# V of a decode attention on a second DMA ring, and gate/up spread on VectorE

## The chip, the core and the metric

The kernel runs on one core of a Trainium2 chip. The metric is the device time of one execution in microseconds (us). A core has TensorE (PE) for matrix products into PSUM, VectorE (DVE), ScalarE (ACT), GpSimd (POOL) and SyncE (SP), each with its own queue of instructions, worked off in order. Transfers between HBM and the on-chip SBUF are issued as instructions of SP, ACT or POOL; each of the three has a ring of its own (q1, q10 and q0 in the profile), and all rings are served by the core's 16 DMA engines.

## The reference

One token (B = 1, Sq = 1) passes attention over a long cache and a gated feed-forward network, side by side; their sum is added to the input. All data are float32.

```python
xn = layernorm(x)                                   # x: (1, 1, 576)
q  = (xn @ wq) as 32 heads of 128                   # wq: 576 x 4096
scores = q . k_cache * 128**-0.5                    # k_cache: 32 heads x 16384 x 128
p  = softmax(scores)
o  = p @ v_cache                                    # v_cache: 32 heads x 16384 x 128
A  = o @ wo                                         # wo: 4096 x 576
g, u = xn @ w_gate, xn @ w_up                       # 576 x 4608 each
B  = (gelu(g) * u) @ w_down                         # w_down: 4608 x 576
out = x + A + B
```

The two caches hold 32 x 16384 x 128 x 4 bytes each, 268 MB; the weights are some 50 MB together.

## The kernel before

**Start.** x is normalized in one row, turned into columns by small matmuls, and copied 32 times side by side (`xnb`, `xtb`), so that `project` (L121) can compute a product in four blocks of 32 partitions: each block of 32 partitions holds the same row, a quarter of the result. wq's product is copied to `qrow`; `q_spread` (L143) spreads q of four heads over all partitions by a matmul with ones, `q_take` (L150) copies it to `qs`, one buffer for four heads. `ffn(0)` and `ffn(1)` (L158) compute gate and up: the product is copied from PSUM to a part of the tile `mix` by ScalarE (L166), and four GpSimd transfers each (L168) bring the four rows into `gu`, 36 values on each of 128 partitions. `ffn_act` (L175) computes gelu(g) * u from `gu` into `hT`.

**Heads.** K and V of one head are a tile of 128 partitions by 16384 values each, 8.39 MB. `kslot` has two buffers, `vslot` has one (L61, L64); `mix` is the first use of `vslot`, so the first V waits until gate and up have left it. All loads are issued by `nc.sync` (L68), on SP's ring, in the order of the loop at L238: K[0] in two halves, K[1], V[0], K[2], V[1], and so on to K[31], V[30]; V[31] goes to a K buffer. A load waits on its issuing queue until its buffer is free: K[h+2] for the DVE work of head h, V[h] for the products of head h-1.

For each head DVE multiplies K by q in place (L204) and sums over the 128 values of each key (L205) into `s`, one buffer. `softmax` (L207) takes the maximum over a partition on DVE (`pm`, L209), transposes it on PE (`pt`, L211), reduces it on DVE (`nm`, L213), spreads it by a matmul (`pb`, L215), copies it on ACT (`nb`, L217), and computes the exponentials on ACT (L218) into `pe`, one buffer. `pv` (L221) multiplies `pe` with V in 32 products on PE (64 matmuls in the trace, as float32 goes in two passes). Every fourth head `out_heads` (L228) gathers four heads: a copy `o4` on ACT, four matmuls, a copy.

What stands in which order on each engine, read from the built program: on PE pv(h-1), then pt(h) and pb(h), then pv(h); on DVE the multiply and the sum of head h, then pm(h), nm(h), then the multiply of head h+1; on ACT nb(h) and exp(h), with `o4` and the `qs` copy between them every fourth head. exp(h) waits for pv(h-1), which reads `pe`; the sum of head h+1 waits for exp(h), which reads `s`.

**End.** wd (36 rows of 576 a partition) is loaded in two pieces, wo (32 rows) in seven, all on SP's ring (L280 to L286). wd's first piece goes to the V buffer and waits for pv(30); its second piece and wo's first go to K[31]'s buffer, the rest of wo to V[31]'s. The output columns are summed in PSUM by `add_out` (L267), in halves of 288 columns and for the last rows in quarters of 144. The normalized heads are transposed by PE and brought to 128 partitions by a GpSimd transfer (`oT`, L299); x is loaded once more by GpSimd (`x2`, L307) and added on DVE. SP stores the result (L323).

Of the kernel before, what the change touches and what calls it, by code (L numbers as in the profile page):

```python
# [8 lines left out]
F32 = mybir.dt.float32  # L9
AF = mybir.ActivationFunctionType  # L10
ALU = mybir.AluOpType
AX = mybir.AxisListType

P = 128
H, SK, DH = 32, 16384, 128
D, DF = 576, 4608
R = SK // P
# [5 lines left out]
HALF = D // 2  # L23
HD = H * DH
QG, QB = HD // 4, 512
QS = HD // 2
FG, FB = DF // 4, 384
WD_T = DF // P
WO_T = HD // P
WD_PIECES = (28, 8)  # L30
WO_PIECES = (14, 8, 5, 2, 1, 1, 1)
WO_A = 14
WO_Q = 10
QUART = D // 4
HG = 4
PW = 4 * HG
# [4 lines left out]
def kernel(ctx: ExitStack, tc: tile.TileContext, x, k_cache, v_cache, wq, wo, wg, wu, wd, out):  # L41
    nc = tc.nc
    cpool = ctx.enter_context(tc.tile_pool(name="cpool", bufs=1))
# [9 lines left out]
    vv = v_cache.rearrange("b h (p n) d -> (b h) p (n d)", p=P)  # L53
    xf = x.rearrange("b s d -> (b s) d")
    of = out.rearrange("b s d -> (b s) d")
    wmain = {n: w[:DM].rearrange("(p j) f -> p (j f)", j=DJ) for n, w in (("q", wq), ("g", wg), ("u", wu))}
    wtail = {n: w[DM:].rearrange("d (s f) -> (d s) f", s=2) for n, w in (("q", wq), ("g", wg), ("u", wu))}
    wov = wo.rearrange("(p t) f -> p (t f)", t=WO_T)
    wdv = wd.rearrange("(p t) f -> p (t f)", t=WD_T)

    def kslot():  # L61
        return kpool.tile([P, R * DH], F32, tag="k", name="kslot")

    def vslot():  # L64
        return vpool.tile([P, R * DH], F32, tag="v", name="vslot")

    def load(dst, src):
        nc.sync.dma_start(dst, src)  # L68
        return dst

    ROW3 = 3 * DF
    wq_t, wg_t, mix = kslot(), kslot(), vslot()
    qt = load(wg_t[:, ROW3 : ROW3 + QS], wtail["q"])
    load(wq_t, wmain["q"])
    row3, tails, at = {}, {}, 0
# [4 lines left out]

    xrow = mix[:1, ROW3 + FG : ROW3 + FG + D]
    nc.scalar.dma_start(xrow, xf)

    ident = cpool.tile([P, P], F32, name="ident")
    make_identity(nc, ident)
# [3 lines left out]
    nc.vector.memset(eps_t, EPS)  # L89
    par = cpool.tile([P, 2], F32, name="par")  # L90
    nc.vector.tensor_reduce(par, ident.rearrange("p (d s) -> p s d", s=2), axis=AX.X, op=ALU.add)
    sel = cpool.tile([P, PW], F32, name="sel")
    nc.vector.tensor_reduce(sel, ident.rearrange("p (q r) -> p r q", q=4)[:, :PW, :], axis=AX.X, op=ALU.add)

    st = cpool.tile([1, 2, nc.vector.BN_STATS_DIM], F32, name="st")
    for i in range(2):
# [21 lines left out]
    xtb = cpool.tile([P, 2, 32], F32, name="xtb")  # L118
    nc.vector.tensor_copy(xtb, xt.unsqueeze(2).to_broadcast([P, 2, 32]))

    def project(steps, group, size):  # L121
        pg = ps_big.tile([P, 3, 512], F32, tag="pb", name="pg")
        for k, (j, rhs) in enumerate(steps):
            for b in range(group // size):
                for q in range(4):
                    lo = q * group + b * size
                    if j < DJ:
                        lhs = xnb[:, j, :]
                    else:
                        lhs = xtb[:, q // 2, :]  # L130
                        lo = (q % 2) * group + b * size
                    nc.tensor.matmul(pg[32 * q : 32 * q + 32, b, :size], lhs, rhs[:, lo : lo + size],  # L132
                                     start=k == 0, stop=k == len(steps) - 1)
        return pg[:, : group // size, :size]

    steps = [(DJ, qt)] + [(j, wq_t[:, j * HD : (j + 1) * HD]) for j in range(DJ)]
    pq = project(steps, QG, QB)
    qrow = cpool.tile([P, QG], F32, name="qrow")
    nc.scalar.activation(qrow.rearrange("p (b f) -> p b f", f=QB), pq, AF.Copy)  # L139

# [2 lines left out]
    def q_spread(h):  # L143
        r = 32 * (h // (H // 4))
        lo = h % (H // 4) * DH
        pq = ps_s.tile([P, 512], F32, tag="sm", name="pq")
        nc.tensor.matmul(pq, ones[r : r + 1, :], qrow[r : r + 1, lo : lo + QH * DH], start=True, stop=True)  # L147
        return pq
# [6 lines left out]

    gu = cpool.tile([P, 2, WD_T], F32, name="gu")

    def ffn(which):  # L158
        n = "gu"[which]
        t = kslot() if which else wg_t  # L160
        steps = [(3, row3[n]), (DJ, tails[n])]
        load(t[:, :ROW3], wmain[n][:, :ROW3])
        steps += [(j, t[:, j * DF : (j + 1) * DF]) for j in range(DJ - 1)]
        gc = mix[:, ROW3 + which * FG : ROW3 + (which + 1) * FG]
        pg = project(steps, FG, FB)
        nc.scalar.activation(gc.rearrange("p (b f) -> p b f", f=FB), pg, AF.Copy)  # L166
        for q in range(4):
            nc.gpsimd.dma_start(gu[32 * q : 32 * q + 32, which, :], gc[32 * q : 32 * q + 1, :])  # L168

    ffn(0)  # L170
    ffn(1)

    hT = cpool.tile([P, WD_T], F32, name="hT")

    def ffn_act():  # L175
        g, u = gu[:, 0], gu[:, 1]
        t1 = cpool.tile([P, WD_T], F32, name="t1")
        tc.keep_in_program_order(nc.vector.tensor_mul(t1, g, g))
        tc.keep_in_program_order(nc.vector.tensor_scalar(t1, t1, 0.044715, 1.0, op0=ALU.mult, op1=ALU.add))
        tc.keep_in_program_order(nc.vector.tensor_mul(t1, t1, g))  # L180
        th = cpool.tile([P, WD_T], F32, name="th")
        nc.scalar.activation(th, t1, AF.Tanh, scale=0.7978845608028654)
        t2 = cpool.tile([P, WD_T], F32, name="t2")
        tc.keep_in_program_order(nc.vector.scalar_tensor_tensor(t2, th, 1.0, g, op0=ALU.add, op1=ALU.mult))
        tc.keep_in_program_order(nc.vector.scalar_tensor_tensor(hT, t2, 0.5, u, op0=ALU.mult, op1=ALU.mult))
# [6 lines left out]
    S, KT, VT = {}, {}, {}  # L192
# [35 lines left out]
    def out_heads(h):  # L228
        o4 = spool.tile([P, 512], F32, name="o4", bufs=1)
        nc.scalar.activation(o4, PO[h // HG % 2], AF.Copy)  # L230
        pc = ps_s.tile([P, 512], F32, tag="sm", name="pc")
        pick = sel.rearrange("p (i j) -> p j i", j=4)
        for j in range(4):
            nc.tensor.matmul(pc[:, :HG], o4[:, j * DH : (j + 1) * DH], pick[:, j, :], start=j == 0, stop=j == 3)  # L234
        nc.scalar.activation(oall[:, h : h + HG], pc[:, :HG], AF.Copy)

    q_take(0, q_spread(0))
    for h in range(H + 1):  # L238
        if h < H:
            KT[h], n = kslot(), R if h else SUB  # L240
            for i in range(0, R, n):
                load(KT[h][:, i * DH : (i + n) * DH], kv[h][:, i * DH : (i + n) * DH])
        if h > 0:
            VT[h - 1] = load(vslot() if h < H else kslot(), vv[h - 1])
        more = (h + 1) % QH == 0 and h + 1 < H
        pq = q_spread(h + 1) if more else None
        if h < H:
            for i in range(0, R, n):
                qk(h, i, n)
            KT.pop(h)  # L250
        if h == 0:
            ffn_act()
        if h > 0:
            pv(h - 1)
            if h % HG == 0:
                out_heads(h - HG)
        if more:
            q_take(h + 1, pq)
        if h < H:
            softmax(h)  # L260
# [19 lines left out]
    ta, tb, te = vslot(), kslot(), kslot()  # L280
    a, b = WD_PIECES
    wd_rows = load_rows(ta, 0, wdv, 0, a) + load_rows(tb, 0, wdv, a, b)
    wo_rows, lo = [], 0
    for n in WO_PIECES:
        wo_rows += load_rows(tb, b + lo, wov, lo, n) if lo < WO_A else load_rows(te, lo - WO_A, wov, lo, n)
        lo += n  # L286
# [4 lines left out]
    nc.vector.reciprocal(rl, pl[:, :H])  # L291
    on = cpool.tile([P, H], F32, name="on")
    nc.vector.tensor_mul(on, oall, rl)
    po = ps_s.tile([P, 512], F32, tag="sm", name="pot")
    nc.tensor.transpose(po[:H, :P], on, ident)
    orow = cpool.tile([H, P], F32, name="orow")
    nc.scalar.activation(orow, po[:H, :P], AF.Copy)
    oT = cpool.tile([P, WO_T], F32, name="oT")
    nc.gpsimd.dma_start(oT, orow)  # L299

    for j, w in enumerate(wd_rows):
        add_out(half[j % 2], hT[:, j : j + 1], w)

    x2 = te[:, R * DH - 2 * HALF : R * DH - HALF]
    nc.vector.memset(x2, 0.0)
    for i in range(2):
        nc.gpsimd.dma_start(x2[32 * i : 32 * i + 1, :], xf[:, i * HALF : (i + 1) * HALF])  # L307

    for j, w in enumerate(wo_rows):
        if j < WO_T - WO_Q:  # L310
            add_out(half[j % 2], oT[:, j : j + 1], w, last=j >= WO_T - WO_Q - 2)
            continue
        if j == WO_T - 5:
            nc.vector.tensor_add(x2[:64], x2[:64], PO[0][64:, :HALF])  # L314
            nc.vector.tensor_add(x2[:64], x2[:64], acc[:64, :HALF])
            for i, g in enumerate(quart):
                r, lo = 32 * (i // 2), i % 2 * QUART
                nc.tensor.matmul(g, ones[r : r + 1, :1], x2[r : r + 1, lo : lo + QUART], start=False, stop=False)
        add_out(quart, oT[:, j : j + 1], w, last=j == WO_T - 1)

    o4 = te[:, R * DH - 3 * HALF : R * DH - 3 * HALF + QUART]
    nc.vector.tensor_copy(o4, acc4)
    nc.sync.dma_start(of.rearrange("o (a f) -> (o a) f", a=4), o4[0:P:32, :])  # L323


# [26 lines left out]
```

## Time and profile before

| | us |
|---|---|
| runs, median of 3 (lowest, highest) | 1370.02 (1369.91, 1370.03) |
| the profiled execution | 1369.89 |
| its span | 1368.1 |
| DVE busy in the span | 1128.3 |
| PE busy | 402.8 |
| ACT busy | 38.9 |
| mean rate of the transfers | 430 GB/s |

The page splits the span into 40 slices and gives the busy share of each engine in tenths; the DMA line is the mean of the 16 DMA engines. Lines of groups name a source line, an engine, the operation, the tiles written and read with their shapes, the count, the busy time and the mean of one in ns, and the idle time before it with what ended it. Lines of the timeline begin with the start and the duration in us. Lines of issues name the queue (SPq is SP's own sequencer), the transfer, its size in KB and the time from issue to landing.

### The profile page before, as it was taken

The numbers are of one execution on the slowest core, as the hardware profiler recorded it, in microseconds if no ns is written. First come the engines' busy times: TensorE is split into PE (matmuls) and PEld (weight loads), VectorE is DVE, ScalarE is ACT, GpSimd is POOL, SyncE is SP. The second block draws the span as 40 slices with busy tenths as digits, with TensorE's granted clock in tenths as the row PEclk, the third lists the DMA queues.
The fourth block names the chain that finished last, engine by engine and source line by source line (L and its number), as shares of the span: only waits on it lengthen the run. The fifth ranks groups of instructions, "written<-read, shape, count | busy, mean of one in ns | idle before, by whom it ended". The sixth has DMA issues, their size and how long they took to land.

```text
span 1368.1 us, 6409 instructions
## 1 busy us (share of the span) xinstructions
PE 402.8 (29%) x2877; PEld 117.2 (9%) x2877; DVE 1128.3 (82%) x160; ACT 38.9 (3%) x128; POOL 6.4 (0%) x17
## 2 busy tenths in 40 slices
PE   4331233322311233322212233322213333222156
PEld 1110000100000000100000000100001000000012
DVE  1059999899888888898888888998888888988840
ACT  0000000000000000000000000000000000000000
POOL 0010000000000000000000000000000000000000
PEclk8775665665566565555565665665566565665577
DMA  9999999999999999999999999999999999999997
GB/s 405 439 423 446 435 431 428 428 439 430 437 437 430 431 428 441 432 433 435 428 439 429 434 431 434 435 430 445 429 430 430 429 439 429 445 428 430 431 431 331
DMA packets 12196, 588.06 MB, mean 430 GB/s; under 512 B 1653, under 2 KB 1673, under 8 KB 2186
## 3 DMA queue, kind: packets, MB, share of 16 engines
q1 hardware_dynamic: 11816, 587.60, 99.4%
q8 instruction: 22, 0.36, 0.1%
q0 software_dynamic: 352, 0.06, 0.0%
q14 instruction: 4, 0.03, 0.0%
q10 hardware_dynamic: 2, 0.00, 0.0%
HBM read 587.60 MB, written 0.00 MB: 429 GB/s over the span
## 4 chain that ended last, share of the span: by engine, by line
DMA 68%; PE 21%; DVE 8%; another core or an unknown queue 1%; issue 1%; ACT 0%; SPq 0%; DVEq 0%; ACTq 0%
DMA vslot<-in_A_v_cache_dram 60%; PE po L225 19%; DVE kslot L204 5%; DVE s L205 3%; DMA vslot<-in_B_w_down_dram 2%; DMA kslot<-in_A_wo_dram 2%; DMA kslot<-in_A_wq_dram 2%; PE pg L132 2%; DMA kslot<-in_A_k_cache_dram 1%; PE pt L211 0%; PE pq L147 0%; ACT qrow L139 0%; DVE pm L209 0%; ACT qs L152 0%
## 5 line engine op out<-in xcount | busy, mean ns | idle before, releaser
L204 DVE TENSOR_TENSOR kslot<-kslot,qs 128x16384 f32<-128x16384 f32 (+1 forms) x33 | 551.3, 16706 | 88.7 <-DMA kslot<-in_A_k_cache_dram 88.7
L205 DVE TENSOR_REDUCE s<-kslot 128x128 f32<-128x16384 f32 (+1 forms) x33 | 551.2, 16703 | 3.3
L225 PE MATMUL po<-vslot,pe 128*16 128x512 f32 x1984 | 282.1, 732 | 645.5 <-DMA vslot<-in_A_v_cache_dram 630.1
L225 PEld LDWEIGHTS po<-vslot,pe 128*16 128x16 f32 x1984 | 66.7, 112 | 845.5 <-issue 828.5
L211 PE MATMUL pt<-ident,pm 128*1 128x128 f32 x32 | 11.9, 372 | 237.4 <-DVE pm L209 237.4
L265 DVE MEMSET acc<- 128x144 f32 x1 | 0.2, 178 | 75.9 <-ACT vslot L166 75.9
L132 PE MATMUL pg<-kslot,xnb 128*32 128x384 f32 (+1 forms) x208 | 24.6, 638 | 35.0 <-DMA kslot<-in_B_w_gate_dram 19.1
L217 ACT ACTIVATE nb<-pb 128x1 f32<-128x1 f32 x32 | 5.5, 172 | 813.4 <-PE pb L215 813.4
L314 DVE TENSOR_TENSOR kslot<-kslot,po 64x288 f32<-64x288 f32 x1 | 0.5, 456 | 29.7 <-PE po L270 29.7
L211 PEld LDWEIGHTS pt<-ident,pm 128*1 128x1 f32 x32 | 2.5, 79 | 260.8 <-DVE pm L209 221.8
L215 PE MATMUL pb<-nm,ones 1*128 1x1 f32 x64 | 18.2, 351 | 13.2 <-DVE nm L213 13.2
L213 DVE TENSOR_REDUCE nm<-pt 1x1 f32<-1x128 f32 x32 | 8.9, 279 | 15.0 <-PE pt L211 15.0
L215 PEld LDWEIGHTS pb<-nm,ones 1*128 1x128 f32 x64 | 15.9, 306 | 22.1 <-DVE nm L213 12.0
L147 PE MATMUL pq<-qrow,ones 1*128 1x512 f32 x16 | 15.6, 1073 | 0.0
L270 PE MATMUL acc<-kslot,oT 128*1 128x144 f32 (+1 forms) x124 | 11.0, 371 | 6.6 <-DMA kslot<-in_A_wo_dram 6.6
L218 ACT ACTIVATE pe<-s,nb 128x128 f32<-128x128 f32 x32 | 12.8, 401 | 1.0
L291 DVE RECIPROCAL rl<-pl 128x32 f32<-128x32 f32 x1 | 0.4, 358 | 14.7 <-PE pl L289 14.7
L132 PEld LDWEIGHTS pg<-kslot,xnb 128*32 128x32 f32 x208 | 7.4, 130 | 52.8 <-DMA kslot<-in_B_w_gate_dram 19.9
L230 ACT ACTIVATE o<-po 128x512 f32<-128x512 f32 x8 | 4.8, 597 | 221.5 <-PE po L225 221.5
L270 PE MATMUL acc<-vslot,hT 128*1 128x288 f32 x56 | 8.4, 464 | 6.5 <-DMA vslot<-in_B_w_down_dram 6.5
L225 PE MATMUL po<-kslot,pe 128*16 128x512 f32 x64 | 9.5, 758 | 2.6 <-DMA kslot<-in_A_v_cache_dram 2.6
L234 PE MATMUL pc<-sel,o 128*128 128x4 f32 x64 | 8.4, 255 | 5.7 <-ACT o L230 5.7
(74 smaller groups left out, 111.1 us busy)
## 6 DMA issues: line engine op xcount, KB each, us to landing
kslot<-in_A_k_cache_dram SPq DMA_DIRECT2D x2, 4096.0 KB, 23.0
vslot<-in_B_w_down_dram SPq DMA_DIRECT2D x1, 8064.0 KB, 29.4
kslot<-in_B_w_gate_dram SPq DMA_DIRECT2D x1, 6912.0 KB, 55.3
kslot<-in_B_w_up_dram SPq DMA_DIRECT2D x1, 6912.0 KB
kslot<-in_A_wo_dram SPq DMA_DIRECT2D x1, 4032.0 KB, 38.0
vslot<-in_B_w_gate_dram SPq DMA_DIRECT2D x1, 2304.0 KB
vslot<-in_B_w_up_dram SPq DMA_DIRECT2D x1, 2304.0 KB, 37.2
kslot<-in_B_w_down_dram SPq DMA_DIRECT2D x1, 2304.0 KB
```

The source lines that it names most:

```text
L132: nc.tensor.matmul(pg[32 * q : 32 * q + 32, b, :size], lhs, rhs[:, lo : lo + size], start=k == 0, stop=k == len(steps) - 1)
L147: nc.tensor.matmul(pq, ones[r : r + 1, :], qrow[r : r + 1, lo : lo + QH * DH], start=True, stop=True)
L204: tc.keep_in_program_order(nc.vector.tensor_mul(blk, blk, Q[h].to_broadcast([P, n, DH])))
L205: nc.vector.tensor_reduce(S[h][:, i : i + n], blk, axis=AX.X, op=ALU.add)
L211: nc.tensor.transpose(pt[:1, :P], pm, ident)
L213: tc.keep_in_program_order(nc.vector.tensor_reduce(nm, pt[:1, :P], axis=AX.X, op=ALU.max, negate=True))
L215: nc.tensor.matmul(pb[:, :1], ones[:1, :], nm, start=True, stop=True)
L217: nc.scalar.activation(nb, pb[:, :1], AF.Copy, scale=SCALE)
L218: nc.scalar.activation(pe4, S.pop(h).rearrange("p (k s) -> p k s", s=4), AF.Exp, bias=nb, scale=SCALE, accum_out=lsum[:, h : h + 1])
L225: nc.tensor.matmul(PO[h // HG % 2][q : q + PW, :], pe[:, lo : lo + PW], vt[:, k * 512 : (k + 1) * 512], start=i == 0 and k < 4, stop=i == ...
L234: nc.tensor.matmul(pc[:, :HG], o4[:, j * DH : (j + 1) * DH], pick[:, j, :], start=j == 0, stop=j == 3)
L270: nc.tensor.matmul(g, lhs, w[:, i * n : (i + 1) * n], start=id(g) not in seen, stop=last)
```

## The change

The function `load` gets the ring as an argument; V of heads 0 to 30 is issued by ScalarE's queue, all other loads stay on SP's. In the built program the issue of V[h] stands on ACT behind exp(h-1) and ahead of nb(h) and exp(h); every fourth one stands behind the copy `o4`, and the `qs` copy of every fourth head stands behind a V issue. V[h] waits for pv(h-1) as before.

Gate and up are no longer copied by ScalarE and moved by GpSimd. A mask `same` (1 where the partition's number within its block of 32 equals the column) is multiplied into the product on DVE, reading PSUM, in blocks of 11, 11 and 10 times 36 columns, and a sum over the blocks on DVE gives `gu`. `oT` is made by a mask `quarter` on DVE and a matmul with `same`. x2 is loaded at the start by two issues on ScalarE into a tile of its own, zeroed by GpSimd. wo is loaded in pieces of 16, 8, 4, 2, 1, 1 rows in place of 14, 8, 5, 2, 1, 1, 1, the quarters take the last 8 rows in place of 10, and the sums of the halves are added 4 rows before the end in place of 5. ScalarE issues the store. GpSimd issues no transfer.

```diff
-WO_PIECES = (14, 8, 5, 2, 1, 1, 1)
-WO_A = 14
-WO_Q = 10
+WO_PIECES = (16, 8, 4, 2, 1, 1)
+WO_A = 16
+WO_Q = 8
...
-    def load(dst, src):
-        nc.sync.dma_start(dst, src)
+    def load(dst, src, ring=nc.sync):
+        ring.dma_start(dst, src)
...
+    x2 = cpool.tile([P, HALF], F32, name="x2")
+    nc.gpsimd.memset(x2, 0.0)
+    for i in range(2):
+        nc.scalar.dma_start(x2[32 * i : 32 * i + 1, :], xf[:, i * HALF : (i + 1) * HALF])
...
-        gc = mix[:, ROW3 + which * FG : ROW3 + (which + 1) * FG]
         pg = project(steps, FG, FB)
-        nc.scalar.activation(gc.rearrange("p (b f) -> p b f", f=FB), pg, AF.Copy)
-        for q in range(4):
-            nc.gpsimd.dma_start(gu[32 * q : 32 * q + 32, which, :], gc[32 * q : 32 * q + 1, :])
+        gm = mix[:, ROW3 : ROW3 + FG].rearrange("p (m t) -> p m t", t=WD_T)
+        at = 0
+        for b, size in enumerate(FB):
+            m = size // WD_T
+            nc.vector.tensor_mul(gm[:, at : at + m, :], pg[:, b, :size].rearrange("p (m t) -> p m t", t=WD_T),
+                                 same[:, at : at + m].unsqueeze(2).to_broadcast([P, m, WD_T]))
+            at += m
+        nc.vector.tensor_reduce(gu[:, which, :], gm.rearrange("p m t -> p t m"), axis=AX.X, op=ALU.add)
...
-            VT[h - 1] = load(vslot() if h < H else kslot(), vv[h - 1])
+            VT[h - 1] = load(vslot() if h < H else kslot(), vv[h - 1], nc.scalar if h < H else nc.sync)
...
-    nc.tensor.transpose(po[:H, :P], on, ident)
-    orow = cpool.tile([H, P], F32, name="orow")
-    nc.scalar.activation(orow, po[:H, :P], AF.Copy)
+    nc.tensor.matmul(po[:, :WO_T], onx, same, start=True, stop=True)
     oT = cpool.tile([P, WO_T], F32, name="oT")
-    nc.gpsimd.dma_start(oT, orow)
+    nc.scalar.activation(oT, po[:, :WO_T], AF.Copy)
...
-    nc.sync.dma_start(of.rearrange("o (a f) -> (o a) f", a=4), o4[0:P:32, :])
+    nc.scalar.dma_start(of.rearrange("o (a f) -> (o a) f", a=4), o4[0:P:32, :])
```

More of the change, by code (lines that the diff above doesn't have):

```diff
@@ L26 @@
 QS = HD // 2
-FG, FB = DF // 4, 384
 WD_T = DF // P
+FG = DF // 4
+FB = (11 * WD_T, 11 * WD_T, 10 * WD_T)
 WO_T = HD // P
 WD_PIECES = (28, 8)
-WO_PIECES = (14, 8, 5, 2, 1, 1, 1)
-WO_A = 14
-WO_Q = 10
+WO_PIECES = (16, 8, 4, 2, 1, 1)
+WO_A = 16
+WO_Q = 8
 QUART = D // 4
@@ L91 @@
     nc.vector.tensor_reduce(par, ident.rearrange("p (d s) -> p s d", s=2), axis=AX.X, op=ALU.add)
-    sel = cpool.tile([P, PW], F32, name="sel")
-    nc.vector.tensor_reduce(sel, ident.rearrange("p (q r) -> p r q", q=4)[:, :PW, :], axis=AX.X, op=ALU.add)
+    same = cpool.tile([P, 32], F32, name="same")
+    nc.vector.tensor_reduce(same, ident.rearrange("p (q r) -> p r q", q=4), axis=AX.X, op=ALU.add)
+    quarter = cpool.tile([P, 4], F32, name="quarter")
+    nc.vector.tensor_reduce(quarter, ident.rearrange("p (q r) -> p q r", q=4), axis=AX.X, op=ALU.add)
     st = cpool.tile([1, 2, nc.vector.BN_STATS_DIM], F32, name="st")
@@ L119, with project @@
     nc.vector.tensor_copy(xtb, xt.unsqueeze(2).to_broadcast([P, 2, 32]))
-    def project(steps, group, size):
+    def project(steps, group, sizes):
         pg = ps_big.tile([P, 3, 512], F32, tag="pb", name="pg")
         for k, (j, rhs) in enumerate(steps):
-            for b in range(group // size):
+            for b, size in enumerate(sizes):
                 for q in range(4):
-                    lo = q * group + b * size
+                    lo = q * group + sum(sizes[:b])
                     if j < DJ:
@@ L130, in project @@
                         lhs = xtb[:, q // 2, :]
-                        lo = (q % 2) * group + b * size
+                        lo -= q // 2 * 2 * group
                     nc.tensor.matmul(pg[32 * q : 32 * q + 32, b, :size], lhs, rhs[:, lo : lo + size],
                                      start=k == 0, stop=k == len(steps) - 1)
-        return pg[:, : group // size, :size]
+        return pg
     steps = [(DJ, qt)] + [(j, wq_t[:, j * HD : (j + 1) * HD]) for j in range(DJ)]
-    pq = project(steps, QG, QB)
+    pq = project(steps, QG, (QB, QB))[:, :2, :]
     qrow = cpool.tile([P, QG], F32, name="qrow")
@@ L231, in out_heads @@
         pc = ps_s.tile([P, 512], F32, tag="sm", name="pc")
-        pick = sel.rearrange("p (i j) -> p j i", j=4)
+        pick = same[:, :PW].rearrange("p (i j) -> p j i", j=4)
         for j in range(4):
@@ L293 @@
     nc.vector.tensor_mul(on, oall, rl)
+    onx = te[:, R * DH - 2 * P : R * DH - P]
+    nc.vector.tensor_mul(onx.rearrange("p (h r) -> p h r", r=4), on.unsqueeze(2).to_broadcast([P, H, 4]), quarter.unsqueeze(1).to_broadcast([P, H, 4]))
     po = ps_s.tile([P, 512], F32, tag="sm", name="pot")
-    nc.tensor.transpose(po[:H, :P], on, ident)
-    orow = cpool.tile([H, P], F32, name="orow")
-    nc.scalar.activation(orow, po[:H, :P], AF.Copy)
+    nc.tensor.matmul(po[:, :WO_T], onx, same, start=True, stop=True)
     oT = cpool.tile([P, WO_T], F32, name="oT")
-    nc.gpsimd.dma_start(oT, orow)
+    nc.scalar.activation(oT, po[:, :WO_T], AF.Copy)
     for j, w in enumerate(wd_rows):
         add_out(half[j % 2], hT[:, j : j + 1], w)
[L304 to L307, printed above, removed]
     for j, w in enumerate(wo_rows):
@@ L312 @@
             continue
-        if j == WO_T - 5:
+        if j == WO_T - 4:
             nc.vector.tensor_add(x2[:64], x2[:64], PO[0][64:, :HALF])
```

## The prediction

> **What bounds the kernel now.** I read the page first: the busy shares, the 40 slices, the queues. The slices show what runs all the time; the queue table shows how the bytes get there.
>
> ```profile
> span 1368.1 us, 6409 instructions
> DVE  1059999899888888898888888998888888988840
> DMA  9999999999999999999999999999999999999997
> ...
> q1 hardware_dynamic: 11816, 587.60, 99.4%
> q0 software_dynamic: 352, 0.06, 0.0%
> q10 hardware_dynamic: 2, 0.00, 0.0%
> ```
>
> The transfer engines are full from the first slice to the last but one, and all of it is q1, SP's ring (q10 is ScalarE's, q0 GpSimd's). VectorE comes next. So the time is bytes over rate, as long as the ring never runs dry. One head as the timeline shows it, with the issues of SP in it:
>
> ```profile
> 1240.12 17.23 DVE L204 TENSOR_TENSOR kslot<-kslot,qs 128x16384 f32<-128x16384 f32 x1 [3.08 <-DMA kslot<-in_A_k_cache_dram]
> 1257.46 17.22 DVE L205 TENSOR_REDUCE s<-kslot 128x128 f32<-128x16384 f32 x1
> 1259.59 9.48 PE L225 MATMUL po<-vslot,pe 128*16 128x512 f32 x64 [21.91 <-DMA vslot<-in_A_v_cache_dram]
> 1269.12 0.33 SPq L68 DMA_DIRECT2D vslot<-in_A_v_cache_dram  x1
> 1274.71 0.33 SPq L68 DMA_DIRECT2D kslot<-in_A_v_cache_dram  x1
> 1274.71 0.29 DVE L209 TENSOR_REDUCE pm<-s 128x1 f32<-128x128 f32 x1
> 1275.05 0.37 PE L211 MATMUL pt<-ident,pm 128*1 128x128 f32 x1 [5.99 <-DVE pm L209]
> 1275.46 0.28 DVE L213 TENSOR_REDUCE nm<-pt 1x1 f32<-1x128 f32 x1 [0.47 <-PE pt L211]
> 1276.62 0.40 ACT L218 ACTIVATE pe<-s,nb 128x128 f32<-128x128 f32 x1
> 1278.82 17.23 DVE L204 TENSOR_TENSOR kslot<-kslot,qs 128x16384 f32<-128x16384 f32 x1 [3.08 <-DMA kslot<-in_A_k_cache_dram]
> 1298.29 8.90 PE L225 MATMUL po<-vslot,pe 128*16 128x512 f32 x64 [21.91 <-DMA vslot<-in_A_v_cache_dram]
> ```
>
> A head lasts 1298.29 - 1259.59 = 38.70 us. K and V are 8.39 MB each (128 rows of 16384 x 4 B), so the ring gives 433.5 GB/s and one tensor alone takes w = 19.35 us. DVE needs 17.23 + 17.22 + 0.1, **34.6 us** a head, and the softmax's way over PE (pm, pt, nm) 1.1 us. The single V buffer is busy with pv, landing to release, for p = 9.2 us (8.4 to 9.9 in the chain of waits). On one ring that gap costs nothing: K[h+1] stands behind V[h] in SP's queue, its bytes fill the gap, and the next V is queued long before they end. **The order on the one ring covers the gap.** Note the 5.99 us that PE waits for pm: pv(h-1) ends 5.6 us before the reduction of head h. That is all the slack V has against DVE, since on PE pt(h) stands behind pv(h-1), and on DVE the next multiply stands behind nm(h), which needs pt(h).
>
> The end of the run, from the timeline and (the wo line) the chain of waits:
>
> ```profile
> 1307.25 0.33 SPq L68 DMA_DIRECT2D vslot<-in_B_w_down_dram  x1
> 1317.63 9.47 PE L225 MATMUL po<-kslot,pe 128*16 128x512 f32 x64 [2.56 <-DMA kslot<-in_A_v_cache_dram]
> 1336.72 27.70 DMA kslot<-in_A_wo_dram
> 1364.96 0.31 DVE L322 COPY kslot<-acc 128x144 f32<-128x144 f32 x1 [4.18 <-PE acc L270]
> 1365.29 0.66 SPq L323 DMA_DIRECT2D out_dram<-kslot  x1
> ```
>
> wd is issued at 1307.25, after pv(30); V[31], landing at 1317.6, covers that. From V[31] to the last wo row 46.8 us pass for 20.05 MB, which are 46.3 at full rate. The profiled execution took 1369.89 us (the median of the runs is 1370.02), so 5.5 us lie behind the last landing at 1364.4.
>
> **The change: V on a second ring.** SP's queue keeps K[0] to K[31], V[31], wd, wo. ScalarE's queue gets V[0] to V[30], each placed behind the exp of the head before and ahead of its own head's nb and exp; it waits for pv of the head before. K no longer stands behind V, nor V behind K. How do two rings share the engines? The trace of before shows it once: the eight small gate/up transfers on q0 while q1 was full (timeline; the view of tile gu; the chain of waits).
>
> ```profile
> 67.18 16.74 SPq L68 DMA_DIRECT2D kslot<-in_A_k_cache_dram  x3
> 83.60 1.13 ACT L166 ACTIVATE vslot<-pg 128x1152 f32<-128x1152 f32 x1 [15.28 <-PE pg L132]
> 85.02 1.97 POOL L168 DMA_DIRECT2D gu<-vslot  x4 [14.27 <-ACT vslot L166]
> 101.63 0.33 SPq L68 DMA_DIRECT2D vslot<-in_A_v_cache_dram  x1
> ...
> DMA to landing us min/median/max: 6.6/9.7/14.9
> ...
> 67.18 18.31 DMA kslot<-in_A_k_cache_dram
> ```
>
> Those of 85.0 to 87.0 landed by 101.6, ahead of K[1], queued at 83.9 behind the second half of K[0] (12.6 MB from 85.5 on, 29 us): not in order of issue. Four of 32 rows are 8 rows on each of 16 engines. In 14.9 us an engine at 433.5/16 = 27.1 GB/s moves eight rows of 32 KB (K[0]'s second half, 9.7 us) and two of 64 KB (4.8): ten of SP's rows for eight of q0's. So I take **one row in turn**. K and V rows are both 64 KB, so each ring gets half. That is an estimate; q10 itself carried 2 packets, too few to show it. The bounds are 0 and 1 for V's share.
>
> The page "DMA: Bandwidth & Descriptors" of the Trainium skill, section "Issuing engines are not separate DMA queues", says that such transfers run on the same 16 engines and interleave, and that a second issuing engine saves issue time only. By it alone the sum would be no change (rival 1); the SP rows above show 0.33 us an issue, already hidden.
>
> From issue to landing I add s = 2.4 us to the bytes, from the smallest full load:
>
> ```profile
> kslot<-in_A_wq_dram SPq DMA_DIRECT2D x1, 1024.0 KB, 4.8
> ```
>
> (4.8 less 2.4 for 1.05 MB.) Rules for the walk: K[h+2] is issued when red(h) ends, V[h] when pv(h-1) ends; a transfer alone moves at full rate, two at half (V[0] against K[0]'s 32 KB rows at 2:1); mul(h) starts at nm(h-1) and K[h] landed; nm(h) 1.1 behind red(h), and 0.7 or more behind pv(h-1); pv takes 9.2. V[0] is free at 87.0: 83.6, three spreads of 0.57, 0.57 and 0.53, a reduction of 1.3, handovers (below). In us:
>
> | h | K landed | red(h) ends | V issued | V landed | pv ends |
> |---|---|---|---|---|---|
> | 0 | 106.7 | 124.1 | 87.0 | 122.3 | 136.8 |
> | 1 | 133.9 | 168.4 | 136.8 | 174.3 | 183.5 |
> | 2 | 167.2 | 204.1 | 183.5 | 216.0 | 225.3 |
> | 3 | 197.9 | 239.8 | 225.3 | 257.8 | 267.0 |
> | 4 | 233.6 | 275.4 | 267.7 | 301.0 | 310.2 |
> | 5 | 269.3 | 311.1 | 310.2 | 350.5 | 359.7 |
> | 6 | 308.8 | 346.7 | 359.7 | 390.1 | 399.3 |
> | 7 | 351.3 | 395.1 | 399.3 | 436.2 | 445.4 |
>
> K runs ahead at DVE's 35.7 us a head; V, sharing, needs 42 and falls behind. V[4] lands at 301 while K[6] is done at 308.8 and K[7] waits for red(5): the engines idle until 312.6, the first 4 us. From head 5 on pv(h-1) ends after red(h), DVE stands behind nm, and two heads repeat:
>
> - long: K[h+2] and V[h] start within some 2 us: V lands s + 2w = 41.1 us after issue, less up to 2; I take 40. Then pv, 9.2, in which the next K has the engines alone.
> - short: that K has had 12.7 us of its 19.35 before V[h+1] moves, 6.7 are left to share, so V lands s + w + 6.7 = 28.4 after issue. Then pv, 9.2, and **nothing to move**: the next K waits for a reduction that began when the long pv ended, 34.6 + 1 us before.
>
> Two heads: 40 + 9.2 + 28.4 + 9.2 + 0.3 (every fourth V stands behind the 0.6 us copy of o4) = 87.1 against 77.4, 9.7 of it idle engines. V[7] goes at 399.3; eleven pairs later V[29] at 1357.4; V[30] at 1406.6, landing 1435.0; pv(30) ends at 1444.2. V[31] has landed long before (SP issues it when red(30) ends, ahead of V[30]), so wd starts uncovered: 2.4 + 46.8 = 1493.4 for the last wo row. With 5.5 behind it: **1499 us**, 129 us over the 1369.9 of the profiled execution.
>
> **The smaller edits** do not touch that sum.
>
> ```profile
> L314 DVE TENSOR_TENSOR kslot<-kslot,po 64x288 f32<-64x288 f32 x1 | 0.5, 456 | 29.7 <-PE po L270 29.7
> 24.87 9.04 PE L132 MATMUL pg<-kslot,xnb 128*32 128x512 f32 x64 [12.55 <-DMA kslot<-in_A_wq_dram]
> ```
>
> Spreading: one DVE multiply of 288 columns from PSUM takes 456 ns and the copy of 144 at the end takes 0.31 us, so about 1.0 ns a column and 0.17 fixed: 0.57, 0.57, 0.53 us; the reduction of 1152 columns at 17.22 us for 16384 is 1.2 plus 0.1. Twice 3 us on DVE in place of two ACT copies of 1.13. The first set hides behind the load of up, the second delays K[0]'s multiply from 85.5 to 86.9; the start is bound by transfers. If that cover were gone it costs 1.4 us. The GpSimd transfers' 14.9 us were late for nothing but V[0]'s issue; V[0] leaves 15 us earlier and takes rows from K[0] and K[1], which land 11 and 19 us later than one ring would land them (95.2, 114.5). That starts the walk, and by itself costs nothing while the engines are full. oT, now by a matmul instead of a transfer, is made when the last pv ends and needed when wo's first rows land, behind 10.6 MB of wd (24 us). The x2 loads add two issues on ScalarE ahead of the square root, the selection tiles 0.6 us on DVE: the projection has 12.55 us of waiting for wq ahead of it. Either costs 0 here, and at most 1.9 (two issues of 0.66 and the 0.6) without that cover. The q copy of every fourth head now stands behind a V issue on ACT, 0.3 us late at 400, seven times. wo in six pieces ends in the same 288 KB row; one issue less lies behind 5 MB queued: -0.4 to 0. The store costs ScalarE what it cost SP, 0.66: between -0.3 and +0.3.
>
> **Rivals.**
>
> 1. *The rings do not share by halves*: V is served first or in order of issue. V keeps up if it lands within 38.7 - 9.2 - 2.4 = 27.1 us of sharing, so from a share of 19.35/27.1 = 0.71 on. Then no lag builds, the order of before comes back, and the time is 1370. For: nothing shows q10 under load. Against: the q0 rows. Chance 0.06.
> 2. *Faster*: as rival 1, and the second ring fills what the one leaves open, 0.6% of the span by q1's 99.4%: 8.2 us, so 1362. It decides from the same 0.71, in the head loop, if the open 0.6% are between transfers. For: two rings can overlap issue and landing (2.4 us). Against: 433.5 GB/s is reached throughout, with no dry stretch to fill. Chance 0.06.
> 3. *Part of it*: V's share between 0.6 and 0.71, or a softer lag. The lag then builds over more heads and the gap is partly covered: between the uncovered wd alone (9.2 + 2.4 = 11.6, so 1381) and two thirds of the gaps, 1455. Chance 0.09.
> 4. *K is favoured*, share under 0.35: the long leg grows towards s + 19.35/0.35 = 57.7 us until K blocks: 1530 to 1590. Chance 0.04.
>
> **How the numbers follow.** The forecast has 0.75. Its own range: gaps of 7 us instead of 9.7 (s of 0.5 instead of 2.4 in each) take 12 x 2.7 = 32 off: 1467; pv at 9.9 instead of 9.2 adds 0.7 x 24 = 17, and a slower shared rate some more: 1525. Held to 8 in 10 with a part of rival 3: 1450 to 1530. A measurement of this kernel tells 0.2% from no change, 2.7 us. Faster is rival 2, 0.06; the same is rival 1, 0.06; slower is the rest, 0.88.
>
> **What would show it.** q10 with 31 V tensors (260 MB); a DMA share of some 0.89 over heads 6 to 30, with dry stretches of 8 to 10 us every second head that begin when a V lands; V's time to landing alternating near 28 and 40; DVE waiting for pt at nm, some 15 us every second head; V[31] landed before V[30], and a dry stretch ahead of wd. The forecast is wrong if V lands in under 27 us every time, or if the DMA slices stay at 9 and 430.

## The result and the profile after

| | us |
|---|---|
| before, median of 4 runs | 1370.01 |
| after, median of 4 runs (lowest, highest) | 1500.32 (1497.86, 1502.82) |
| the profiled execution after | 1502.82 |
| its span | 1501.0 |

The ratio is 1.0951, 95% interval [1.0937, 1.0964]. The forecast was 1499.0 in a range of 1450 to 1530. Slices, queues and three groups of the page after:

```profile
span 1501.0 us, 6360 instructions
...
DVE  1077999995969968687897877789887877888830
DMA  9999999999797997979899898899999898999978
...
q1 hardware_dynamic: 7200, 327.55, 51.7%
q10 hardware_dynamic: 4478, 260.06, 40.1%
...
L215 DVE TENSOR_TENSOR kslot<-kslot,qs 128x16384 f32<-128x16384 f32 (+1 forms) x33 | 550.8, 16690 | 13.0 <-DMA kslot<-in_A_k_cache_dram 9.6
...
L236 PE MATMUL po<-vslot,pe 128*16 128x512 f32 x1984 | 285.5, 740 | 914.7 <-DMA vslot<-in_A_v_cache_dram 914.7
L224 DVE TENSOR_REDUCE nm<-pt 1x1 f32<-1x128 f32 x32 | 8.9, 278 | 223.2 <-PE pt L222 223.2
```

The bytes are the same, 260 MB of them now on q10. The two rings together fill 91.8% of the engines' span (51.7 and 40.1) where the one filled 99.4%. The first ten slices are still full; then sevens and eights come in. DVE's two waits in a head, as the page before has them:

```profile
L204 DVE TENSOR_TENSOR kslot<-kslot,qs 128x16384 f32<-128x16384 f32 (+1 forms) x33 | 551.3, 16706 | 88.7 <-DMA kslot<-in_A_k_cache_dram 88.7
L213 DVE TENSOR_REDUCE nm<-pt 1x1 f32<-1x128 f32 x32 | 8.9, 279 | 15.0 <-PE pt L211 15.0
```

Before, DVE waited 88.7 us in all for K and 15.0 us for pt ahead of nm. Now it waits 223 us for pt, and 13 us ahead of the multiply (L215), 9.6 of them for K. So DVE does not lack K; it waits for its turn behind PE, and PE waits 915 us for V.

A stretch of the loop in steps of 2 us (start:end, length, PE, PEld, DVE, ACT, POOL busy, PE clock, DMA share, GB/s):

```profile
1170.00:1172.00 2.00, 0.00 (x0) 0.00 (x0) 2.00 (x1) 0.00 (x0) 0.00 (x0) 0.50 1.13 492
1172.00:1174.00 2.00, 0.00 (x0) 0.00 (x0) 2.00 (x1) 0.00 (x0) 0.00 (x0) 0.50 0.16 66
1174.00:1176.00 2.00, 0.00 (x0) 0.00 (x0) 2.00 (x1) 0.00 (x0) 0.00 (x0) 0.50 0.00 0
1176.00:1178.00 2.00, 1.85 (x12) 0.56 (x16) 2.00 (x1) 0.00 (x0) 0.00 (x0) 0.50 0.00 0
1178.00:1180.00 2.00, 2.00 (x16) 0.39 (x9) 1.13 (x2) 0.00 (x0) 0.00 (x0) 0.50 0.79 262
```

The timeline of the same place:

```profile
1144.11 0.28 DVE L224 TENSOR_REDUCE nm<-pt 1x1 f32<-1x128 f32 x1 [10.19 <-PE pt L222]
1144.32 17.20 DVE L215 TENSOR_TENSOR kslot<-kslot,qs 128x16384 f32<-128x16384 f32 x1
1161.62 17.22 DVE L216 TENSOR_REDUCE s<-kslot 128x128 f32<-128x16384 f32 x1
1176.15 9.84 PE L236 MATMUL po<-vslot,pe 128*16 128x512 f32 x64 [31.26 <-DMA vslot<-in_A_v_cache_dram]
1178.87 0.33 SPq L69 DMA_DIRECT2D kslot<-in_A_k_cache_dram  x1
1178.88 0.29 DVE L220 TENSOR_REDUCE pm<-s 128x1 f32<-128x128 f32 x1
1185.91 0.27 PE L222 MATMUL pt<-ident,pm 128*1 128x128 f32 x1
1186.05 0.34 ACTq L69 DMA_DIRECT2D vslot<-in_A_v_cache_dram  x1
1186.22 0.28 DVE L224 TENSOR_REDUCE nm<-pt 1x1 f32<-1x128 f32 x1 [7.06 <-PE pt L222]
1186.43 17.20 DVE L215 TENSOR_TENSOR kslot<-kslot,qs 128x16384 f32<-128x16384 f32 x1
```

Read it downwards. The last bytes of V move at about 1172.3 (a share of 0.16 in the stretch from 1172), V has landed by 1176.0, and the K before it too; the engines have nothing. The next V has to wait for pv (to 1185.98); the next K has to wait for the reduction that runs until 1178.8. From 1172.3 to about 1178.9 nothing moves. And the reduction is late because the multiply before it began only at 1144.32, when the pv before had let pt through: nm stood 10.19 us behind pt there, stands 7.06 us behind it here, and pt behind pv. Before, a K stood in the one ring behind every V, and this hole was filled.

### The profile page after: what moved, and what is told of

The parts are those of the page before. It is cut to its first block, busy times and chain, and to the rows that moved or that the text cites. A ratio compares the mean times of both kernels' runs of the same rounds, so it can differ in the third digit from the quotient of the medians.

```text
span 1501.0 us, 6360 instructions
## 1 busy us (share of the span) xinstructions
PE 390.4 (26%) x2870; PEld 112.5 (7%) x2870; DVE 1133.9 (76%) x169; ACT 36.2 (2%) x126; POOL 1.0 (0%) x7
## 3 DMA queue, kind: packets, MB, share of 16 engines
q1 hardware_dynamic: 7200, 327.55, 51.7%
q10 hardware_dynamic: 4478, 260.06, 40.1%
## 4 chain that ended last, share of the span: by engine, by line
DMA 78%; PE 21%; DVE 0%; issue 0%; SPq 0%; ACT 0%; ACTq 0%
DMA vslot<-in_A_v_cache_dram 71%; PE po L236 19%; DMA kslot<-in_B_w_up_dram 3%; DMA kslot<-in_A_wo_dram 3%; DMA kslot<-in_A_wq_dram 2%; PE pg L139 1%; PE acc L281 1%; DVE gu L179 0%; PE pt L222 0%; DVE vslot L176 0%; SPq L69 0%; DVE x L320 0%; DVE x L321 0%; PE acc L324 0%; DVE kslot L328 0%
## 5 line engine op out<-in xcount | busy, mean ns | idle before, releaser
L215 DVE TENSOR_TENSOR kslot<-kslot,qs 128x16384 f32<-128x16384 f32 (+1 forms) x33 | 550.8, 16690 | 13.0 <-DMA kslot<-in_A_k_cache_dram 9.6
L236 PE MATMUL po<-vslot,pe 128*16 128x512 f32 x1984 | 285.5, 740 | 914.7 <-DMA vslot<-in_A_v_cache_dram 914.7
L139 PE MATMUL pg<-kslot,xnb 128*32 128x396 f32 (+2 forms) x208 | 23.8, 620 | 34.6 <-DMA kslot<-in_B_w_gate_dram 19.3
L226 PE MATMUL pb<-nm,ones 1*128 1x1 f32 x64 | 13.2, 272 | 12.6 <-DVE nm L224 12.6
L226 PEld LDWEIGHTS pb<-nm,ones 1*128 1x128 f32 x64 | 10.7, 207 | 19.1 <-DVE nm L224 13.8
L159 ACT ACTIVATE qs<-pq 128x512 f32<-128x512 f32 x8 | 4.8, 597 | 264.7 <-PE pt L222 238.8
L220 DVE TENSOR_REDUCE pm<-s 128x1 f32<-128x128 f32 x32 | 9.1, 286 | 1.1
L245 PE MATMUL pc<-same,o 128*128 128x4 f32 x64 | 8.4, 255 | 5.7 <-ACT o L241 5.7
L154 PE MATMUL pq<-qrow,ones 1*128 1x512 f32 x16 | 9.9, 700 | 0.0
```

Source lines behind the costliest of these rows:

```text
L215: tc.keep_in_program_order(nc.vector.tensor_mul(blk, blk, Q[h].to_broadcast([P, n, DH])))
L220: tc.keep_in_program_order(nc.vector.reduce_max(pm, S[h], axis=AX.X))
L226: nc.tensor.matmul(pb[:, :1], ones[:1, :], nm, start=True, stop=True)
L236: nc.tensor.matmul(PO[h // HG % 2][q : q + PW, :], pe[:, lo : lo + PW], vt[:, k * 512 : (k + 1) * 512], start=i == 0 and k < 4, stop=i == ...
```

## The experiments

The **theory** is that of the prediction: the rings move row for row, V gets half, falls behind, and from then on nothing covers the time in which pv reads the single V buffer. **Rivals**: another edit costs it; two rings cost rate by themselves; ScalarE's in-order queue, in which a waiting V issue holds up the softmax.

### Only the other edits; only the ring

```diff
-            VT[h - 1] = load(vslot() if h < H else kslot(), vv[h - 1], nc.scalar if h < H else nc.sync)
+            VT[h - 1] = load(vslot() if h < H else kslot(), vv[h - 1])
```

> The changed kernel with V back on SP's ring; all its other edits stay. If the second ring alone makes the loss, this is back at 1370, give or take 2 us (the other edits were put at -0.7 to +0.8). If the edits at the start or the end carry a part of the 130 us, that part stays: anything above 1375 would say so.

Measured: 1370.00 us (11 runs), ratio 1.0 [0.9991, 1.0009]. In the kernel before, with only V's ring changed:

```diff
-    def load(dst, src):
-        nc.sync.dma_start(dst, src)
+    def load(dst, src, ring=nc.sync):
+        ring.dma_start(dst, src)
...
-            VT[h - 1] = load(vslot() if h < H else kslot(), vv[h - 1])
+            VT[h - 1] = load(vslot() if h < H else kslot(), vv[h - 1], nc.scalar if h < H else nc.sync)
```

> The kernel before with nothing changed but V of heads 0 to 30 on ScalarE's ring. Theory of the lag (each ring moves half, V's buffer gap is uncovered, DVE stands behind PE): 1490 to 1510, as the whole change. V[0] starts some 15 us later here, at about 102 instead of 87, since gate/up still pass through GpSimd; the walk by the same rules gives 6 us more for that, so about 1505. If the other edits carried the loss: 1370.

Measured: 1513.08 us (one run), 3 us above the range that was expected. The ring is the whole loss; with V on the one ring the other edits come to nothing within 0.1%. This kernel is 13 us slower than the whole change, where 6 were expected for the later start of V[0]. Its chain of waits (V's time from issue to landing, heads 0 to 3):

```profile
101.97 42.05 DMA vslot<-in_A_v_cache_dram
152.99 33.82 DMA vslot<-in_A_v_cache_dram
196.56 42.03 DMA vslot<-in_A_v_cache_dram
248.06 28.29 DMA vslot<-in_A_v_cache_dram
```

V[0] goes at 102 instead of 87, and the pattern of a long and a short wait is there from head 2 on, three heads sooner than after the whole change. Three more heads at some 5 us would be about what it costs; no run moves the start of V[0] alone.

### How the rings share: K in halves, K in thirds

```diff
             KT[h], n = kslot(), R if h else SUB
-            for i in range(0, R, n):
-                load(KT[h][:, i * DH : (i + n) * DH], kv[h][:, i * DH : (i + n) * DH])
+            kn = min(n, R // 2)
+            for i in range(0, R, kn):
+                load(KT[h][:, i * DH : (i + kn) * DH], kv[h][:, i * DH : (i + kn) * DH])
```

> The changed kernel with each K loaded in two transfers of 8192 columns, so that SP's rows are 32 KB against V's 64 KB. If the rings take one row in turn, V gets two thirds; that is just under the 0.71 from which V keeps up, and the walk by the prediction's rules gives about 1418. If the rings share by bytes whatever the row, or if two rings simply cost rate, or if the loss comes from V's issue standing in ScalarE's queue: 1500 as before.

Measured: 1455.79 us (one run). In thirds the loop reads

```diff
+            cuts = (0, 43, 86, R) if h else (0, SUB, R)
+            for i, e in zip(cuts, cuts[1:]):
+                load(KT[h][:, i * DH : e * DH], kv[h][:, i * DH : e * DH])
```

> The changed kernel with each K loaded in three transfers of 43, 43 and 42 keys a partition, rows of 21.5 KB. One row in turn gives V three quarters, over the 0.71: no lag, no dry stretch, 1367 to 1371. If two rings cost rate by themselves (contention), it stays above 1370 by that cost, seen as a rate under 433 GB/s in a stretch without dry spells. If the rings share by bytes, or the place in ScalarE's queue makes the loss: 1500.

Measured: 1384.60 us (4 runs), ratio 1.0104 [1.0091, 1.0118]. Its control, one ring and K in thirds:

> Control for the kernel with K in thirds on two rings (1384.6 us, no dry stretch, 427 GB/s): the same three transfers for each K, but V back on SP's ring. If rows of 21.5 KB are themselves slower, it is 1383 to 1387 and the second ring costs nothing once V keeps up. If it is the taking of turns between two rings that costs rate, this is back at 1370 to 1372.

Measured: 1375.34 us (4 runs), ratio 1.0038 [1.0023, 1.0053]. That lies between the two times expected of it, so each of the two causes seems to have a part.

Shorter rows on K's ring take a third of the loss away in halves and nine tenths in thirds, so the share is not by bytes. The queues in a stretch in which both rings had work (packets, MB, share), first after the change (1188 to 1208 us), then with K in halves (139 to 160 us):

```profile
q1 hardware_dynamic: 71, 4.65, 53.7%
q10 hardware_dynamic: 64, 4.19, 48.4%
```

```profile
DMA packets 209, 9.40 MB, mean 448 GB/s; under 512 B 16, under 2 KB 16, under 8 KB 16
q10 hardware_dynamic: 94, 6.16, 67.8%
q1 hardware_dynamic: 115, 3.24, 35.9%
```

After the change every packet is a row: 71 rows against 64 of the same length. With K in halves 16 of the 209 packets are under 512 B and no rows; 3.24 MB are 99 rows of 32 KB, so it is 99 rows against 94. V's share of the bytes is 0.47 and 0.66. That it is one row in turn shows in shorter windows. By an estimate from 433.5 GB/s over 16 engines a row of 64 KB takes one engine 2.4 us, and after the change the windows of 2.4 us from 1189.0 to 1208.2 hold 16 rows of q10, then 16 of q1, and so on, eight times without an exception. The first two:

```profile
q10 hardware_dynamic: 16, 1.05, 100.8%
q1 hardware_dynamic: 16, 1.05, 100.8%
```

The loop at 440 to 1240 us, in thirds on two rings and in thirds on one:

```profile
440.00:1240.00 800.00, 223.94 (x1457) 62.28 (x1457) 710.25 (x84) 20.86 (x78) 0.00 (x0) 0.61 1.00 427
```

```profile
440.00:1240.00 800.00, 222.34 (x1454) 61.44 (x1454) 719.22 (x82) 20.21 (x75) 0.00 (x0) 0.61 1.00 430
```

The expectations for halves and thirds both missed on the slow side. With thirds, 5.3 us of the 14.6 are there on one ring already (430 in place of 433 GB/s); the other 9.3 come with the second ring (427), at a DMA share of 1.00 and thus without dry stretches. In halves the walk was 38 us short. V there takes 30 to 32 us from issue to landing in heads 2 to 6, as two thirds gives (2.4 + 29), still over the 27.1, so a lag did have to build. From V's issue at 464.7 us to the one at 1356.2 it then takes near 33 us, and a head 42.5 us, where the walk's rules have 40.6 (31.4 + 9.2). Why V takes longer there is not settled.

### ScalarE's queue

```diff
-            VT[h - 1] = load(vslot() if h < H else kslot(), vv[h - 1], nc.scalar if h < H else nc.sync)
+            VT[h - 1] = load(vslot() if h < H else kslot(), vv[h - 1], nc.gpsimd if h < H else nc.sync)
```

> The changed kernel with V of heads 0 to 30 issued by GpSimd, on q0, in place of ScalarE. ScalarE's queue holds no V issue any more, so if the softmax standing behind V's issue makes the loss, this is 1370 to 1385. If it is the lag (two rings by halves, a V buffer that leaves its ring empty while it is read), the queue that issues does not matter: 1490 to 1515.

Measured: 1508.21 us (one run), inside the range of the lag. The queue, and the loop after the change and in this kernel:

```profile
q0 software_dynamic: 4464, 260.05, 39.9%
```

```profile
440.00:1240.00 800.00, 196.41 (x1323) 53.31 (x1323) 638.35 (x74) 18.66 (x71) 0.00 (x0) 0.60 0.91 387
440.00:1240.00 800.00, 195.69 (x1323) 53.43 (x1315) 631.21 (x74) 18.88 (x71) 10.02 (x19) 0.60 0.90 386
```

The 260 MB went over q0, ScalarE issued none of it, and the loop runs at 386 GB/s where the change had 387. The place of the V issue in ScalarE's queue is not the cause.

### The gap itself

V in two transfers, with the buffer released as a whole:

```diff
-            VT[h - 1] = load(vslot() if h < H else kslot(), vv[h - 1], nc.scalar if h < H else nc.sync)
+            VT[h - 1] = vslot() if h < H else kslot()
+            vn = R // 2 if h < H else R
+            for i in range(0, R, vn):
+                load(VT[h - 1][:, i * DH : (i + vn) * DH], vv[h - 1][:, i * DH : (i + vn) * DH], nc.scalar if h < H else nc.sync)
```

> The changed kernel with each V loaded in two transfers of 32 KB rows, on ScalarE's ring; the buffer is still released as a whole. K in halves gave V 0.615 of the shared bytes, so V should get 0.385 here. pv's first half runs when the first half lands, so the ring stands empty for 4.6 + 2.4 us instead of 9.2 + 2.4. A smaller share with a smaller gap: by the walk's rules 1450 to 1495. Theory of ScalarE's queue: 1500 or above, as the queue is blocked longer.

Measured: 1467.20 us (one run), inside the expected range. The share of 0.615 in that expectation is less than the 0.66 read above; by one row in turn V in halves gets a third, not 0.385. And with one tile for all heads, so that each half is released when it has been read:

```diff
+            if h == 1:
+                vbig = vslot()
+            VT[h - 1], ring = (vbig, nc.scalar) if h < H else (kslot(), nc.sync)
+            for i in (0, SUB):
+                load(VT[h - 1][:, i * DH : (i + SUB) * DH], vv[h - 1][:, i * DH : (i + SUB) * DH], ring)
```

> As the kernel with V in two transfers, but all heads write one and the same V tile, so that the first half is released when pv has read it and the next head's first half is issued while the second is still being read. Sharing, rows, rings and queues are as there; only the gap in which V's ring has nothing goes. If the uncovered gap is the loss, the engines never run dry and this is 1370 to 1386 (the upper end if taking turns costs the rate seen with K in thirds). If sharing itself or ScalarE's queue is the loss: 1450 or above, as the kernel with V in two transfers.

Measured: 1377.03 us (4 runs), ratio 1.0051 [1.0034, 1.0068]. The loop of the first and of the second kernel, and of the kernel before:

```profile
440.00:1240.00 800.00, 232.71 (x1331) 55.07 (x1335) 670.45 (x78) 18.94 (x71) 0.00 (x0) 0.63 0.94 401
```

```profile
440.00:1240.00 800.00, 252.15 (x1422) 58.80 (x1422) 717.89 (x82) 20.15 (x75) 0.00 (x0) 0.65 1.00 432
```

```profile
440.00:1240.00 800.00, 225.05 (x1457) 62.47 (x1457) 719.90 (x84) 20.81 (x78) 0.00 (x0) 0.61 1.00 433
```

Transfers, rows, rings and issuing queue are the same in both, but for V[31], which goes in two pieces in the second. Only the moment at which half a buffer comes free differs, and with it go 90 us and the dry stretches: 432 GB/s, as on one ring (433). Two rings that share by rows, V still the slower one, cost next to nothing in the loop once V's ring always holds a transfer. **The uncovered gap is the loss.** Of the 7 us that remain, about half are behind by the end of the loop. Moved by 1300 us, in the kernel before and in this one:

```profile
DMA packets 10686, 561.97 MB, mean 432 GB/s; under 512 B 1409, under 2 KB 1409, under 8 KB 1410
DMA packets 14872, 560.37 MB, mean 431 GB/s; under 512 B 1635, under 2 KB 1637, under 8 KB 1638
```

1.6 MB are 3.7 us at 433 GB/s. The rest comes behind it, where from 1317 to 1321 us little moves: there the wd load, still waiting for V's buffer (until 1320.9), finds no K behind it.

No kernel here beats the one before: all move the same 588 MB, and its one ring was never dry.

## Why the prediction was right

**The share.** It was put at one row in turn, so half, from the eight small transfers on q0; measured 71 rows to 64, and row by row in the windows of 2.4 us. This held for q10, and for q0 with large rows (V by GpSimd, 140 to 160 us: 64 rows to 66 on q1).

**The walk.** The chain of waits after (start, us, what):

```profile
136.20 36.24 DMA vslot<-in_A_v_cache_dram
172.58 9.90 PE po L236 x64
182.50 34.28 DMA vslot<-in_A_v_cache_dram
...
312.83 41.53 DMA vslot<-in_A_v_cache_dram
354.50 9.36 PE po L236 x64
363.92 27.99 DMA vslot<-in_A_v_cache_dram
392.04 9.36 PE po L236 x64
401.46 38.84 DMA vslot<-in_A_v_cache_dram
...
1230.33 33.40 DMA vslot<-in_A_v_cache_dram
1263.86 8.65 PE po L236 x64
1272.58 34.41 DMA vslot<-in_A_v_cache_dram
...
1360.40 33.62 DMA vslot<-in_A_v_cache_dram
```

V[1] goes at 136.2 (the table has 136.8), V[5] at 312.8 (310.2), V[6] at 363.9 (359.7), V[7] at 401.5 (399.3). The first nm that waits for pv is that of head 5 (2.1 us in place of 0.5), the first long wait that of head 6 (16.0). The prediction says head 5; in its table pv(4) ends 0.9 us ahead of red(5), which makes it head 6.

**The pair.** From V[7] at 401.46 to V[29] at 1360.40 eleven pairs take 958.9 us, 87.2 each; 87.1 was predicted. But not in the form predicted: the long and the short leg (41.5 and 28.0 at heads 5 and 6) draw together and are both 33 to 34 by the end, with a shorter dry stretch in every head (6.6 us in the one shown) in place of a long one in every second. DVE's wait at nm is accordingly 7 to 10 us a head late in the run, 16 only at the start.

The prediction's own rules say why the sum of two heads does not mind. If K is issued x ahead of V, V lands 41.1 - x after its issue; pv takes 9.2 more, and DVE's next reduction ends 35.3 after the pv before (0.7 + 34.6). So the next x is 15.0 - x, and two neighbours add up to the same whatever the split. On the trace x shows as DVE's wait at nm: 16.0 and 2.5 at heads 6 and 7, 10.2 and 7.1 at 1144 and 1186 us, 18.5 and 17.3 in sum. One long and one short leg was only one of the splits that the rules allow, and with V by GpSimd the legs end far apart (41.5 and 27.5 from 1274.7 us on). What moves the split was not tried. That the mean comes out within 0.1 us is luck: single pairs take 85.3 to 88.5 us, and from issue to landing V takes up to 3 us more than the rules give (41.5 in place of 38.9 at V[5], where x was 2.2), which longer leads of K make up for.

**The end.** V[31] goes at 1395.3, ahead of V[30] (1402.6), and wd uncovered, after a stretch from about 1435.2 us in which nothing moves (timeline):

```profile
1438.31 8.47 PE L236 MATMUL po<-vslot,pe 128*16 128x512 f32 x64 [34.85 <-DMA vslot<-in_A_v_cache_dram]
1446.84 0.33 SPq L69 DMA_DIRECT2D vslot<-in_B_w_down_dram  x1
```

Predicted for the issue of wd 1444.2, measured 1446.84; the execution ended 3.9 us later than the sum, 2.6 of it here.

**The small edits.** They were put at nothing and came to nothing (the one-ring kernel). Of their sizes one was off: the second reduction of gate/up takes 2.18 us, not 1.3. It reads its 1152 columns with a stride of 36, while the 1.3 came from a reduction that reads side by side; no run shows that the stride is the reason. The three spreads together take 1.50 us instead of 1.67, the start is 0.1 earlier and the handovers are shorter, so V[0] went at 87.23 where 87.0 was put.

**Rivals 1 and 2** needed a share of 0.71. The kernel with K in thirds goes past it (8.39 of 11.39 MB, 0.74, from 850 to 876 us) and indeed has no lag (DVE waits 15.0 us in all for pt, as before), but stays 1% over 1370: the one mechanism that was to end on the fast side, a second ring filling what the first leaves open, found nothing to fill. Here the trace agrees with the Trainium skill's page "DMA: Bandwidth & Descriptors", section "Issuing engines are not separate DMA queues", that rings started by several engines interleave on the same 16 engines: 433 GB/s on one ring, 427 to 432 on two that do not run dry. What it says of the saving, issue time, was 0.33 us an issue and hidden. "No change" did not follow from it, since the second ring also undid the order that covered the gap.

**Rival 3**, a share of 0.6 to 0.71, is the kernel with K in halves (0.66): 1455.8 us, at the slow end of the 1381 to 1455 that were put for it.

## What to carry to other kernels

A single ring is also a schedule: a load queued behind another covers the time in which the first one's buffer is read. Before moving a stream to a ring of its own, work out its cycle at the shared rate (bytes over half the rate where the rows of both rings are equally long, plus issue to landing, plus the time its buffer is held) and compare it with the loop's. If it is longer, as here, the stream falls behind until its consumer's queue, here DVE behind PE, stalls the other stream as well. The remedy that worked here is a buffer released in parts, so that the ring always holds the next transfer; shorter rows on the other ring, which raise the stream's share, helped too.

## What the runs showed of the hardware

Two busy rings took turns by rows, not by bytes: 16 rows of one, then 16 of the other, in windows of 2.4 us, and 99 rows of 32 KB to 94 of 64 KB. K in rows of 64, 32 and 21.5 KB beside V rows of 64 KB gave 1500, 1456 and 1385 us with nothing else changed. K in three transfers with rows of 21.5 KB took 0.4% more time on one ring, and a second ring beside them 0.7% more (430 and 427 GB/s in the loop, against 433), while 32 KB rows of V beside 64 KB rows of K ran at 432.
